# Eight special dk stores instead of five, with their rows dealt to chosen DMA engines

## The chip, the cores and the metric

The kernel runs on one core of one Trainium2 chip. The core has a matrix engine (PE, with weight loads shown apart as PEld), three engines for elementwise work (DVE, ACT, POOL), a synchronising engine (SP) and 16 DMA engines that move data between HBM and the on-chip memory. The metric is the time of one execution in microseconds (us); lower is better. Before the change it was 1268.67 us, the median of 3 runs from 1267.47 to 1269.34 us.

## The reference

The computation is the decode step of attention with its gradients, for 2 x 32 = 64 heads. A head has one query row of 128, and 8192 rows of keys and of values, all in bf16.

```python
scale = q.shape[-1] ** -0.5
scores = einsum("bhqd,bhkd->bhqk", q, k) * scale      # q (2,32,1,128), k and v (2,32,8192,128)
p = softmax(scores, axis=-1)
out = einsum("bhqk,bhkd->bhqd", p, v)
dq, dk, dv = vjp(out)(grad_out)
```

Written out for one head, with g the row of grad_out: dv is the outer product of p and g; dS = p * (V g - sum(p * V g)); dq is scale * dS K; dk is the outer product of dS and scale * q. So K and V (2 MB each for a head) are read once, and dK and dV (2 MB each) are written once: 256 transfers of 2 MB in all, nearly 537 MB.

## The kernel before

**Tiles.** A head's K, and its V, is one on-chip tile of 128 partitions with 64 rows of 128 numbers in each: 16,384 bytes a partition, contiguous in HBM. There are 12 such buffers, six heads deep. `load` (L106) brings a tile in on SP's DMA queue. The tile is read by PE and then overwritten in place by its own gradient: `outer` (L469) writes a quarter of it at a time with one DVE instruction (L475, a quarter is 16 of the 64 rows of each partition), and after the last quarter the tile is stored to dk or dv. The load for the head six places on, into the same buffer, waits for that store to land.

**Order of the work.** One loop (L506) makes eight steps a head, four quarters of K and then four of V, and interleaves up to four heads: transposes and scores of one head, softmax and sums of the one before, the outer products of the one before that. The order on every engine is pinned by hand. Within a head the dV quarters come first and the dK quarters right behind them.

**Queues.** Loads go out on SP's queue (q1 in the profile, hardware descriptors). Stores of whole tiles go out on POOL's queue (q0, software descriptors); only those of the last head go, a quarter at a time, on SP's. The final `out` and `dq` rows go on SP's (L585). In the trace the loads count their landings on eight semaphores in turn and POOL's DMAs on eight others, and a DMA whose semaphore is still owed a landing is not issued until that has come. A DMA posts sixteen landings, one an engine.

**Special stores.** Five of the 64 dk stores, those of heads 6, 17, 28, 39 and 50 (`SPREAD`, L23), are not sent as one DMA. `by_rows` (L96) sends partitions 8 to 127 first (120 rows of 16,384 bytes, with an upper bound on the length of the innermost piece, "cut") and then partitions 0 to 2, 3 to 5 and 6 to 7 (uncut). After the dv store of the next head, `turn` (L88) is called twice (`BACK`, L524): `turn(0)` resets a cursor of POOL's DMA queue, and `turn(5)` issues a tiny DMA of 5 rows of 16 bytes into a scrap tile (`parts_all`). The same is done once at the start (L128): a reset, and the first 5 query rows on POOL's queue. The cursor says on which DMA engine the next cut DMA of this queue begins.

**What the change touches** are the tables `SPREAD` and `BACK` at L23 to L26, the count of scrap tiles `NTURN` at L120 and the two calls of `turn` at L525 and L526.

Of the kernel before, what the change touches and what calls it, by code (L numbers as in the profile page):

```python
# [19 lines left out]
SW = 32  # L20
NTILE = 12
FIRST = 5
SPREAD = {  # L23
    i: ((8, 128, True), (0, 3, False), (3, 6, False), (6, 8, False)) for i in range(6, 56, 11)
}
BACK = {i + 1: FIRST for i in SPREAD}  # L26

@with_exitstack
def kernel(  # L30
# [57 lines left out]
    def turn(n):  # L88

        if n:  # L90
            parts = turns.pop()
            pin(store_eng.dma_start(out=parts[:n, :], in_=q_rows[:n, : 2 * QT], max_dma_last_dim=2 * QT))
        else:
            pin(store_eng.inc_swdge_sem([], [], mode="reset_dge_cursor"))

    def by_rows(dst, src, steps):  # L96

        for step in steps:
            if len(step) == 1:
                turn(*step)  # L100
                continue
            p0, p1, cut = step
            cap = {"max_dma_last_dim": NT * D} if cut else {}
            pin(store_eng.dma_start(out=dst[p0:p1], in_=src[p0:p1], **cap))

    def load(i, w, pieces=(NCH,)):  # L106
        h = heads[i]
        t = kvp.tile([P, NT, D], BF16, tag=f"kv{slot_of(i, w)}", name="kvt")
        h.tile[w] = t
        src = (v_v if w else k_v)[i]  # L110
        c = 0
        for m in pieces:
            n0, n1 = c * CH, (c + m) * CH
            pin(load_eng.dma_start(out=t[:, n0:n1, :], in_=src[:, n0:n1, :]))
            c += m
# [1 line left out]
    load(0, 0, (1, 1, 2))  # L117

    q_rows = q.rearrange("b h s d -> (b h s) d")
    NTURN = len(BACK) + sum(len(step) == 1 and step[0] > 0 for x in SPREAD.values() for step in x)  # L120
    parts_all = const.tile([CH, NTURN, 2 * QT], BF16, name="parts_all")
    turns = [parts_all[:, n, :] for n in range(NTURN)]

    qd_nat = evp.tile([P, CH, P], BF16, tag="ev", name="qd_nat")
    for w, a in enumerate((q, grad_out)):
        rows = a.rearrange("b h s d -> (b h s) d")
        r0 = FIRST if w == 0 else 0
        if r0:  # L128
# [73 lines left out]
    def begin(i):  # L202

        h = heads[i]
        sw = ps_sdp.tile([P, 2 * NT + 2 * P + 4], F32, tag="s", name="sw")
        h.score = (sw[:, 0:NT], sw[:, NT : 2 * NT])
        h.s, h.dp = h.score
        h.mT = sw[0:1, 2 * NT : 2 * NT + P]
        h.qbp = sw[:, 2 * NT + P : 2 * NT + 2 * P]
        h.lsum = sw[:, 2 * NT + 2 * P : 2 * NT + 2 * P + 2]  # L210
        h.mb = sw[:, 2 * NT + 2 * P + 2 : 2 * NT + 2 * P + 3]

    def window(i, w):

        pin(nc.scalar.copy(out=qwin[:, w, :, Q0 : Q0 + 2], in_=qpair[:, w, i]))

    def broadcast(i, w):

        h = heads[i]
        pin(  # L220
            nc.tensor.matmul(  # L221
                h.qbp,
                lhsT=qT[:, w, i : i + 1].to_broadcast([P, P]),
                rhs=ident_bf,
                start=True,
                stop=True,
            )
        )
        h.qb[w] = small.tile([P, D], BF16, tag=f"qb{w}", name="qb")
        pin(nc.vector.tensor_copy(out=h.qb[w][:], in_=h.qbp))  # L230

    def transpose_chunk(i, c):
        w, c = divmod(c, NCH)
        src = heads[i].tile[w]
        tp = ps_tp.tile([P, CH // 2, P], F32, tag="tp", name="tp")
        for m in range(CH // 2):
            n0 = c * CH + 2 * m
            two = src[:, n0 : n0 + 2, :].rearrange("p n d -> p (n d)").bitcast(F32)
            pin(nc.tensor.transpose(tp[:, m, :], two, ident_f[:]))  # L239
        ev = evp.tile([P, CH // 2, P], F32, tag="ev", name="ev")  # L240
        pin(nc.scalar.copy(out=ev[:], in_=tp[:]))  # L241
        return ev
# [26 lines left out]
    def keep_raw(i):  # L269

        h = heads[i]
        h.rows = work.tile([P, QT * P], F32, tag="rows", name="rows")
        pin(nc.vector.tensor_copy(out=h.rows[:], in_=h.raw[:]))  # L273
# [179 lines left out]
    def join(i, w):  # L453

        h = heads[i]
        pin(
            nc.tensor.matmul(h.acc[w][:, 0:1], lhsT=h.sel[:], rhs=ones[:], start=True, stop=True)  # L457
        )
        pin(
            nc.vector.tensor_scalar(  # L460
                out=(oT if w else dqT)[:, i : i + 1],
                in0=h.acc[w][:, 0:1],
                scalar1=h.rl if w else h.rls,
                scalar2=None,
                op0=ALU.mult,
            )
        )

    def outer(i, w, c, ends):  # L469

        h = heads[i]
        n0 = c * CH
        shape = [P, CH, D // 2, 2]
        pin(
            nc.vector.tensor_tensor(  # L475
                out=h.tile[w][:, n0 : n0 + CH, :].rearrange("p n (e t) -> p n e t", t=2),
                in0=h.qb[w][:]
                .rearrange("p (e t) -> p e t", t=2)
                .unsqueeze(1)
                .to_broadcast(shape),  # L480
                in1=h.pair[w][:, n0 : n0 + CH, :].unsqueeze(2).to_broadcast(shape),
                op=ALU.mult,
            )
        )
        if c + 1 in ends:
            at = ends.index(c + 1)
            b0, b1 = (ends[at - 1] if at else 0) * CH, (c + 1) * CH
            dst = (dv_v if w else dk_v)[i]
            if w == 0 and i in SPREAD:
                by_rows(dst, h.tile[w], SPREAD[i])  # L490
            else:
                eng = load_eng if len(ends) > 1 else store_eng
                pin(eng.dma_start(out=dst[:, b0:b1, :], in_=h.tile[w][:, b0:b1, :]))  # L493
# [12 lines left out]
    for g in range(SL * BH + O0 + NCH + 4 - SL):  # L506
        now = [(g // SL - b, g % SL + b * SL) for b in range(4)]
        now = [(i, r) for i, r in now if 0 <= i < BH]

        def at(r0):  # L510

            return next((i for i, r in now if r == r0), None)

        def within(r0):

            return next(((i, r - r0) for i, r in now if r0 <= r < r0 + NCH), None)

        if (i := at(O1 + NCH)) is not None and i + AHEAD < BH:
            load(i + AHEAD, 0)
        if (i := at(O0 + NCH)) is not None and i + AHEAD < BH:  # L520
            load(i + AHEAD, 1)
        if x := within(O1):
            outer(x[0], 1, x[1], last if x[0] == BH - 1 else whole)
        if (i := at(O1 + NCH)) in BACK:  # L524
            turn(0)  # L525
            turn(BACK[i])  # L526
        if x := within(O0):
            outer(x[0], 0, x[1], last if x[0] == BH - 1 else whole)
        ev = None
        if g < SL * BH:  # L530
            i, r = divmod(g, SL)
            if r == NCH:
                begin(i)
                broadcast(i, 1)
            if r == NCH + 2:
                broadcast(i, 0)
            ev = transpose_chunk(i, r)
        if (i := at(A1 + NCH + 2)) is not None:
            join(i, 1)
        if (i := at(A0 + NCH + 2)) is not None:  # L540
            join(i, 0)
        if x := within(A1):
            acc(x[0], 1, x[1])
        if x := within(A0):
            acc(x[0], 0, x[1])
        if (i := at(NCH + 1)) is not None:
            spread_rows(i, 0)
        if (i := at(SL + 1)) is not None:
            spread_rows(i, 1)
        if (i := at(NCH + 3)) is not None:  # L550
            max_spread(i)
            expo(i)
        if prev is not None:
            score_chunk(*prev)
        prev = (g // SL, g % SL, ev) if ev is not None else None
        if (i := at(NCH + 1)) is not None and i + 1 < BH:
            window(i + 1, 0)
        if (i := at(1)) is not None and i > 0:
            window(i, 1)

        if (i := at(NCH)) is not None:
            keep_raw(i)
        if (i := at(SL)) is not None:
            keep_raw(i)
        if (i := at(NCH + 1)) is not None:
            max_part(i)
        if (i := at(NCH + 2)) is not None:
            max_all(i)
        if (i := at(NCH + 4)) is not None:
            normalise_p(i)  # L570
        if (i := at(SL + 1)) is not None:
            weigh(i)
        if (i := at(SL + 2)) is not None:
            normalise_ds(i)
        if (i := at(A1 + NCH)) is not None:
            pick(i, 1)
        if (i := at(A0 + NCH)) is not None:
            pick(i, 0)
# [37 lines left out]
```

## Time and profile before

| | |
|---|---|
| runs | 1268.67 us (median of 3; 1267.47 to 1269.34) |
| profiled execution, its own time | 1267.85 us |
| its span, first to last instruction | 1266.1 us |
| busy: PE, DVE, ACT, POOL | 1187.7, 1031.3, 557.2, 80.6 us |
| bytes moved by DMA, mean rate | 538.53 MB, 425 GB/s |
| DMA packets on POOL's queue, on SP's queue | 19456, 20172 |
| mean granted clock of PE | 0.988 of full speed |

The page lists first how long every engine was busy. Then it cuts the span into 40 equal slices and shows for each the busy share in tenths, the granted PE clock, the mean busy share of the 16 DMA engines and what they moved in GB/s. Then come the DMA queues; the chain of work that ended last; the costliest groups of instructions, with the idle time before them and what ended it; and the DMA issues by line, with their size and the median time from issue to landing. Other views give the waits of each engine, the instructions of a stretch in order of time, and tables by stretch, in which the DMA share is a fraction of 1 (packets overlap by some nanoseconds, so that it can show 1.01). Behind the views stand the records of the trace: start, length, size and queue of every DMA packet, and the time of every landing. They don't name the engine, but an engine's packets follow one another without a break, so that each engine can be followed as a chain of packets.

### The profile page before, as it was taken

The page shows a single profiled execution, that of the slowest core. Times are in us where ns is not written, and L with a number is a line of the kernel's source. Part 1 is how long each engine was busy: PE and PEld are TensorE (multiplying, and loading weights), DVE is VectorE, ACT ScalarE, POOL GpSimd, SP SyncE. Part 2 cuts the span into 40 slices and gives each one's busy share as a digit, 9 for nine tenths or more (in the row PEclk, how much of TensorE's full clock was granted, in tenths as well). Part 3 has the DMA queues.
Part 4 walks back from the last instruction along what each step waited for, and adds up shares of the span by engine and source line. Part 5 has one row for each costly group of instructions (what it writes and reads, how often), then busy time and mean ns, then how long its engine had stood idle before and what let it go on. Part 6 is the DMA issues. An engine that isn't in the chain of part 4 may idle for free.

```text
span 1266.1 us, 24581 instructions
## 1 busy us (share of the span) xinstructions
PE 1187.7 (94%) x10056; PEld 783.1 (62%) x10056; DVE 1031.3 (81%) x2267; ACT 557.2 (44%) x769; POOL 80.6 (6%) x153
## 2 busy tenths in 40 slices
PE   6999999999999999999999999999999999999981
PEld 4666666666666666666666666666666666666650
DVE  3888888888888888888888888888888888887883
ACT  3444444444444444444444444444444444444430
POOL 0000010000010000001000001000000001000000
PEclk9999999999999999999999999999999999999995
DMA  9999999999999999999999999999999999999998
GB/s 393 422 429 429 429 428 429 429 429 429 430 429 428 429 429 429 429 429 429 423 428 430 430 429 428 428 427 430 429 430 428 429 429 427 429 429 429 429 430 336
DMA packets 39741, 538.53 MB, mean 425 GB/s; under 512 B 5236, under 2 KB 5236, under 8 KB 6516
## 3 DMA queue, kind: packets, MB, share of 16 engines
q1 hardware_dynamic: 20172, 272.70, 50.6%
q0 software_dynamic: 19456, 264.25, 49.1%
q8 instruction: 79, 1.29, 0.4%
q14 instruction: 34, 0.28, 0.1%
HBM read 268.47 MB, written 268.47 MB: 424 GB/s over the span
## 4 chain that ended last, share of the span: by engine, by line
PE 68%; DVE 16%; DMA 7%; another core or an unknown queue 4%; issue 2%; ACT 0%; SPq 0%; POOL 0%; ACTq 0%; DVEq 0%
PE tp L239 29%; PE acc L420 17%; PE raw L260 11%; DVE kvt L475 6%; PE sw L280 4%; DMA out_dram<-kvt 4%; DVE sel L443 4%; DVE rows L273 3%; DMA kvt<-in_v_dram 3%; PE sw L366 3%; PE sw L221 2%; PE sw L304 1%; DVE sel L437 1%; PE acc L457 1%
## 5 line engine op out<-in xcount | busy, mean ns | idle before, releaser
L241 ACT COPY ev<-tp 128x1024 f32<-128x1024 f32 x512 | 518.7, 1013 | 660.3 <-PE tp L239 654.8
L475 DVE TENSOR_TENSOR kvt<-qb,pair 128x2048 bf16<-128x2048 bf16 x512 | 617.2, 1216 | 0.2
L239 PE MATMUL tp<-ident_f,kvt 128*128 128x128 f32 x4096 | 547.6, 277 | 3.1 <-DMA kvt<-in_v_dram 2.6
L239 PEld LDWEIGHTS tp<-ident_f,kvt 128*128 128x128 f32 x4096 | 454.0, 144 | 84.2 <-issue 64.6
L260 PE MATMUL raw<-ev,qwin 128*32 128x512 bf16 x2048 | 209.5, 399 | 0.0
L420 PE MATMUL acc<-kvt,dS_pad 128*64 128x512 bf16 x1024 | 160.7, 395 | 0.8 <-DVE dS_pad L406 0.8
L420 PE MATMUL acc<-kvt,E_pad 128*64 128x512 bf16 x1024 | 159.5, 391 | 0.6 <-DVE E_pad L331 0.6
L280 PEld LDWEIGHTS sw<-sel,rows 128*128 128x128 f32 x1024 | 123.9, 191 | 52.4 <-DVE sel L443 25.9
L443 DVE SCALAR_TENSOR_TENSOR sel<-acc,diag,sel 128x128 f32<-128x128 f32 x384 | 134.7, 351 | 13.6
L260 PEld LDWEIGHTS <-qwin 128*32 128x32 bf16 x2048 | 52.7, 93 | 135.4 <-issue 131.0
L280 PE MATMUL sw<-sel,rows 128*128 128x16 f32 x1024 | 136.3, 265 | 0.0
L493 POOL DMA_DIRECT2D out_dram<-kvt x121 | 64.6, 533 | 1062.3 <-DVE kvt L475 484.4
L273 DVE COPY rows<-raw 128x512 f32<-128x512 f32 x128 | 88.6, 692 | 47.0 <-PE raw L260 47.0
L299 DVE TENSOR_REDUCE st<-sw 1x1 f32<-1x128 f32 x64 | 17.8, 278 | 55.9 <-PE sw L298 55.9
L221 PE MATMUL sw<-ident_f,qT 128*128 128x128 bf16 x128 | 28.9, 226 | 36.2 <-DVE st L294 36.2
L420 PEld LDWEIGHTS <-dS_pad 128*64 128x64 bf16 x1024 | 36.6, 108 | 34.9 <-issue 31.8
L366 PEld LDWEIGHTS sw<-st,ones 128*128 128x128 f32 x256 | 37.9, 186 | 31.0 <-issue 15.3
L420 PEld LDWEIGHTS <-E_pad 128*64 128x64 bf16 x1024 | 36.0, 108 | 33.6 <-issue 31.5
L366 PE MATMUL sw<-st,ones 128*128 128x1 f32 x256 | 48.8, 260 | 0.5 <-DVE st L337 0.5
L437 DVE TENSOR_SCALAR sel<-acc,diag 128x128 f32<-128x128 f32 x128 | 43.8, 342 | 0.0
L457 PEld LDWEIGHTS acc<-ones,sel 128*128 128x128 f32 x256 | 39.0, 193 | 7.2 <-DVE sel L443 7.2
L457 PE MATMUL acc<-ones,sel 128*128 128x1 f32 x256 | 36.7, 212 | 6.1 <-DVE sel L443 6.1
(54 smaller groups left out, 381.3 us busy)
## 6 DMA issues: line engine op xcount, KB each, us to landing
out_dram<-kvt POOLq DMA_DIRECT2D x121, 2048.0 KB, 44.9
kvt<-in_v_dram SPq DMA_DIRECT2D x64, 2048.0 KB, 20.1
kvt<-in_k_dram SPq DMA_DIRECT2D x63, 2048.0 KB, 20.2
out_dram<-kvt POOLq DMA_DIRECT2D x5, 1920.0 KB, 49.5
out_dram<-kvt SPq DMA_DIRECT2D x8, 512.0 KB, 20.1
kvt<-in_k_dram SPq DMA_DIRECT2D x2, 512.0 KB, 4.4
kvt<-in_k_dram SPq DMA_DIRECT2D x1, 1024.0 KB, 6.9
out_dram<-kvt POOLq DMA_DIRECT2D x10, 48.0 KB, 49.1
```

What stands on the lines that cost most here:

```text
L239: pin(nc.tensor.transpose(tp[:, m, :], two, ident_f[:]))
L241: pin(nc.scalar.copy(out=ev[:], in_=tp[:]))
L260: nc.tensor.matmul(h.raw[g * SW : (g + 1) * SW, :], lhsT=qwin[:, w, e, q0 : q0 + SW], rhs=cols[:, b, :, e], start=(c == 0), stop=(c == NCH ...
L273: pin(nc.vector.tensor_copy(out=h.rows[:], in_=h.raw[:]))
L280: nc.tensor.matmul(h.score[w].rearrange("p (n m t) -> p n m t", m=QT, t=2)[:, :, m, :], lhsT=h.rows[:, m * P : (m + 1) * P], rhs=sel4[:].r ...
L366: nc.tensor.matmul(out, lhsT=ones[:].to_broadcast([P, P]), rhs=col, start=True, stop=True)
L420: nc.tensor.matmul(h.acc[w][g : g + CW, :], lhsT=wts[:, n0 : n0 + CW], rhs=rows[:, n0 : n0 + QT, :].rearrange("p n d -> p (n d)"), start=( ...
L437: nc.vector.tensor_scalar(out=h.sel[:], in0=block, scalar1=diag[:, 0:1], scalar2=None, op0=ALU.mult)
L443: nc.vector.scalar_tensor_tensor(out=h.sel[:], in0=block, scalar=diag[:, b : b + 1], in1=h.sel[:], op0=ALU.mult, op1=ALU.add,)
L457: nc.tensor.matmul(h.acc[w][:, 0:1], lhsT=h.sel[:], rhs=ones[:], start=True, stop=True)
L475: nc.vector.tensor_tensor(out=h.tile[w][:, n0 : n0 + CH, :].rearrange("p n (e t) -> p n e t", t=2), in0=h.qb[w][:] .rearrange("p (e t) -> ...
L493: pin(eng.dma_start(out=dst[:, b0:b1, :], in_=h.tile[w][:, b0:b1, :]))
```

## The change

Eight dk stores are special, those of heads 6, 14, 22, 29, 35, 41, 47 and 53. They come in four forms. Heads 6 and 22 keep the old form. Heads 14 and 41 send 120 rows, a scrap DMA of 4 rows, and the other 8 rows as one cut DMA. Heads 29, 35 and 47 send 104 rows, a scrap DMA of 4, 15 or 11 rows, 17 rows as one cut DMA, and the last 7 rows as uncut pieces of 3, 3 and 1. Head 53 sends 104 rows and three uncut pieces of 8. After the following head's dv store there is a scrap DMA of a listed number of rows (none after head 53); the reset of the cursor is left in one place, behind head 6. The description of the change gives the aim: four stores as 120 rows without engine 4, four as 104 rows without three neighbouring engines, and the 17 rows on engine 7, 8 or 15.

```diff
+SMALL = ((0, 3, False), (3, 6, False), (6, 8, False))
+REST = ((17, 20, False), (20, 23, False), (23, 24, False))
 SPREAD = {
-    i: ((8, 128, True), (0, 3, False), (3, 6, False), (6, 8, False)) for i in range(6, 56, 11)
+    6: ((8, 128, True),) + SMALL,
+    14: ((8, 128, True), (4,), (0, 8, True)),
+    22: ((8, 128, True),) + SMALL,
+    29: ((24, 128, True), (4,), (0, 17, True)) + REST,
+    35: ((0, 104, True), (15,), (104, 121, True), (121, 124, False), (124, 127, False), (127, 128, False)),
+    41: ((8, 128, True), (4,), (0, 8, True)),
+    47: ((24, 128, True), (11,), (0, 17, True)) + REST,
+    53: ((0, 104, True), (104, 112, False), (112, 120, False), (120, 128, False)),
 }
-BACK = {i + 1: FIRST for i in SPREAD}
+BACK = {7: (0, 5), 15: (5,), 23: (2,), 30: (4,), 36: (12,), 42: (7,), 48: (15,)}
...
-    NTURN = len(BACK) + sum(len(step) == 1 and step[0] > 0 for x in SPREAD.values() for step in x)
+    NTURN = sum(n > 0 for x in BACK.values() for n in x) + sum(
+        len(step) == 1 and step[0] > 0 for x in SPREAD.values() for step in x
+    )
...
         if (i := at(O1 + NCH)) in BACK:
-            turn(0)
-            turn(BACK[i])
+            for n in BACK[i]:
+                turn(n)
```

## The prediction

> **What bounds the kernel now.** I read the busy slices and the DMA queues first.
>
> ```profile
> span 1266.1 us, 24581 instructions
> ...
> DMA  9999999999999999999999999999999999999998
> GB/s 393 422 429 429 429 428 429 429 429 429 430 429 428 429 429 429 429 429 429 423 428 430 430 429 428 428 427 430 429 430 428 429 429 427 429 429 429 429 430 336
> ...
> q1 hardware_dynamic: 20172, 272.70, 50.6%
> q0 software_dynamic: 19456, 264.25, 49.1%
> ```
>
> The DMA engines are busy in every slice and move 428 to 430 GB/s in nearly all; PE is the next fullest with 94%. Then the table by stretch, for the end:
>
> ```profile
> core 0: us, PE busy (x) PEld busy (x) DVE busy (x) ACT busy (x) POOL busy (x), PEclk, DMA share, GB/s
> 1000.00:1020.00 20.00, 19.43 (x168) 12.90 (x168) 17.02 (x37) 8.70 (x13) 1.06 (x2) 1.00 1.01 430
> 1020.00:1040.00 20.00, 19.43 (x168) 13.07 (x168) 17.02 (x39) 8.86 (x13) 0.64 (x1) 1.00 1.00 427
> 1040.00:1060.00 20.00, 19.43 (x168) 12.59 (x165) 16.77 (x37) 9.53 (x13) 1.09 (x2) 1.00 1.01 428
> 1060.00:1080.00 20.00, 19.43 (x168) 12.99 (x169) 16.85 (x40) 8.69 (x12) 2.65 (x5) 1.00 1.01 426
> ...
> 1220.00:1240.00 20.00, 14.81 (x112) 8.39 (x110) 17.38 (x39) 4.05 (x6) 0.54 (x2) 0.86 1.01 429
> 1240.00:1266.00 26.00, 3.36 (x14) 1.55 (x14) 6.25 (x12) 0.00 (x0) 0.00 (x0) 0.50 0.76 318
> ```
>
> All 16 engines work until 1240 us and only the last stretch has room (share 0.76), when PE and DVE have nothing left that matters. So the end is set by the DMA engine that finishes its own share last. How far apart do they finish? The landing records answer: a DMA posts one landing an engine, and those of the first `out_dram<-nat` transfer (16 KB behind everything else) came at 1251.0, 1251.6, 1251.8 | 1257.2 | 1259.8, 1259.8 | 1262.0, 1262.5, 1262.8, 1262.8, 1263.0, 1263.2, 1263.4, 1263.5, 1263.6, 1264.9 us. Their mean is 1260.2. The same bytes, dealt perfectly, would end 1264.9 - 1260.2 = 4.7 us earlier: that is all that dealing can win (0.37%).
>
> **Who is who.** An engine's packet of one row (16,384 bytes) is followed by the next 0.607 us after its start, in both queues; two half packets of a cut row take the same. So a row more or less is 0.607 us of an engine's end. At each old special store the packet records show fifteen engines with sixteen half rows, one with none, and three engines with one whole row from each uncut piece (two of them three rows in all, the third two), always among the five that also get a row of the 5-row scrap DMA. Row n of a scrap or uncut DMA therefore sits on engine n from its beginning, uncut ones begin at engine 0, and a cut DMA begins at the cursor and moves it on by the engines it used. Over the run the old tables moved 5 x 8 = 40 rows off engine 4 and put 15, 15 and 10 on engines 0, 1 and 2. That dates their ends: 15 x 0.607 = 9.1 and 10 x 0.607 = 6.1 us above the leading three at 1251.0 to 1251.8 gives 1260.1 to 1260.9 and 1257.1 to 1257.9, where the pair at 1259.8 and the single at 1257.2 are. So six engines have one natural speed: 0, 1, 2 and three that lead because they were given nothing. Ten are about 11 us slower over the run, engine 4 by some 24 us more, which its 40 rows repair. The records name a reason in part: the 79 instruction packets (q8, 1.29 MB) go round eight engines in turn, and in the stretches where I could follow them never to the three leaders. The names of these three are not in the trace: they are three of 5 to 15.
>
> **The change, part by part.** Following the cursor from 5: head 6 omits engine 4 as before; 14 omits 4 and puts one row each on 8 to 15; 22 omits 4; 29 omits 3, 4, 5 and puts 17 rows on 7; 35 omits 9, 10, 11 and puts 17 on 8; 41 is as 14; 47 omits 4, 5, 6 and puts 17 on 15; 53 omits 12, 13, 14 and puts three rows each on 0 to 7. These agree with the description of the change. Against the kernel before, in rows: engine 0 +3, 1 none, 2 +3, 3 -5, 4 -5, 5 -13, 6 -5, 7 +20, 8 +19, each of 9 to 14 -6, 15 +19; the sum is nought.
>
> Suppose 7, 8 and 15 are the three leaders. Then they end at 1251.0 to 1251.8 + 19 or 20 x 0.607 (11.5 or 12.1) = 1262.5 to 1263.9. The slow ten lose at least 5 rows, 3.0 us: at most 1261.9. Engines 0 and 1: at most 1259.8 + 1.8 = 1261.6. The leaders have become the last, about 4 us behind the mean of the ten, because 17 rows is more than the 13 or so that would level them.
>
> Empty shares: engines left out of a cut DMA still show a 4-byte packet for each piece they miss (the omitted engine of the old stores shows sixteen), 6 ns each. A 17-row DMA is 34 pieces, so 0.2 us for the others, three times; the leaders meet two of these, 0.4 us. The last end is then 1262.9 to 1264.3, say 1263.8 against 1264.9: 1.1 us less.
>
> POOL's issues: before, 20 special DMAs, 5 scrap DMAs and 5 resets; after, 36 within the special stores, 7 scrap DMAs behind them and 1 reset, while three whole stores more are replaced. That is 15 DMAs more at 0.51 to 0.64 us, under 10 us of POOL, which idles most of the span:
>
> ```profile
> POOL out_dram L493 <- DVE kvt L475: 484.4, 51, 13.4
> POOL out_dram L493 <- DVE qb L230: 475.5, 54, 34.3
> ...
> POOL out_dram L493 <- DMA out_dram<-kvt: 36.1, 4, 12.3
> POOL parts_all L92 <- DMA out_dram<-kvt: 25.8, 3, 8.9
> ...
> POOL out_dram L104 <- DMA out_dram<-kvt: 13.0, 3, 9.2
> ```
>
> The last three lines are what the issues do cost: a special store makes five DMAs of two, POOL's eight semaphores run out, and the stores behind wait for a landing (the queue's in order, so all of POOL's later stores, and through them SP's loads into those buffers, move back). At head 50 the following dk store went out at 1041.4 instead of about 1016.6 us. Yet the table above shows 426 to 430 GB/s there: each store takes 43.3 us (median) from issue to landing, so enough is queued. At heads 29, 35 and 47 the event has seven DMAs, two landings more, at 9.7 us each: about 25 + 19 = 44 us late, as long as the queue lasts. I take nothing for it; the ends are 0 (a store is still queued) and 2 us of idleness a time, 6 us in all. The fewer resets and 16-byte rows I take at nothing: a scrap DMA's packet is some 10 ns on an engine, times 12.
>
> Sum: -1.1 + 0, about 1267.85 - 1.1 = 1266.7 for a profiled execution; from the median of runs, 0.8 above it, 1267.6.
>
> **A rule against it.** The trace shows three engines of 5 to 15 ahead and doesn't name them. The Trainium skill, DMA: Bandwidth & Descriptors, section Latency and other measured facts, says that engines 7 and 15 are usually slower than 0-6 and 8-14; no row here shows that. By it, this change would load two of the slow ten, and the sum would be that of the first rival.
>
> **The rivals.** (1) *An engine fed 17 rows isn't a leader.* Then it ends at 1262.0 to 1264.9 + 11.5 or 12.1, that is 1273.5 to 1277.0, or 8.6 to 12.1 us later than now: 1277 to 1281, and any one of the three is enough. It decides as soon as one of them has now less than about 9 us of lead over the last (1264.9 + 2.5 - 11.6 = 1255.8). For it: nothing in the records names them. Against: engine 4 and engines 0 to 2 were treated by the old tables just as the ends call for, and ten engines are slow, exactly as many as the new table relieves (3 to 6, 9 to 14). (2) *POOL's semaphores starve the stores*, as priced: up to 6 us, 1267.6 to 1274, slower by over 0.2% from about 4 us on. Against it, the full rate around 1040 us. (3) *The 17 rows are not confined to one engine* but fall two by two on 0 to 8: engines 0 to 7 get six, engine 4 then -39 against -40, the last end moves by +0.6 us: about 1269.3. Against it, 120 and 5 rows went just where the cursor says. (4) *A better level*: if an ordinary run has the leaders further ahead than the profiled one, up to the 4.7 us: 1264 to 1266.
>
> **How the numbers follow.** 0.2% is 2.5 us, about what a measurement of this kernel can tell from no change. The forecast gets 0.57, rival 3 0.03 (both within 0.2%), rival 1 0.20, rival 2 0.07, rival 4 0.13. So faster 0.13, same 0.60, slower 0.27. The likeliest has 1266.0 to 1270.0 of its own; to leave out no more than 0.2 the range goes down to 1264.3 and up to 1278.0, into rival 1.
>
> **What would show it.** Right: three engines' landings of the last transfers move from 13 us ahead to the end of the field, the ten come 3 to 4 us earlier (engine 5 some 8), the spread shrinks from 13.9 to 5 to 9 us, and the share in the last stretch rises while the span shrinks by about 1 us. Wrong by rival 1: one to three landings stand some 10 us behind the rest. Wrong by rival 2: a slice between 640 and 1080 us falls under 420 GB/s, POOL waits over 20 us for a landing.

## The result and the profile after

The changed kernel takes 1282.02 us (median of 5 runs, 1281.36 to 1285.62) against 1267.47 us (5 runs, 1267.33 to 1269.34): a ratio of 1.0116, 95% interval 1.0100 to 1.0132. It is 14.5 us slower where 1.1 us less was forecast for the profiled execution and 1267.6 us for the median. The profiled execution has an own time of 1281.36 us and a span of 1279.6 us, 13.5 us more than before. The first lines to read are again the DMA slices and the queues:

```profile
span 1279.6 us, 24600 instructions
...
DMA  9999999999999999999999999999999899999997
GB/s 396 417 428 430 429 429 428 430 429 428 428 428 430 428 430 426 429 431 427 425 406 427 429 423 401 430 427 431 427 431 418 339 428 432 426 426 426 431 427 324
...
q1 hardware_dynamic: 20172, 272.70, 50.2%
q0 software_dynamic: 21936, 264.26, 48.9%
```

Each slice is 32.0 us. In the first twenty the rates are those of before; then there are four holes, 406, 401, 418 and 339 GB/s, in the slices that begin at 640, 768, 960 and 992 us. The bytes are the same, so the holes are lost time. The table by stretch (columns as before: busy time of each engine, granted clock, DMA share, GB/s) narrows them down:

```profile
640.00:660.00 20.00, 19.43 (x168) 12.87 (x166) 17.01 (x39) 9.07 (x13) 2.69 (x5) 1.00 0.95 389
...
760.00:780.00 20.00, 19.43 (x168) 12.75 (x166) 16.98 (x38) 8.90 (x13) 2.24 (x5) 1.00 0.98 404
780.00:800.00 20.00, 19.43 (x169) 13.00 (x165) 16.94 (x39) 9.55 (x14) 2.04 (x4) 1.00 0.99 399
...
1000.00:1020.00 20.00, 19.43 (x169) 12.56 (x167) 17.01 (x36) 9.20 (x13) 3.79 (x7) 1.00 0.78 303
1020.00:1040.00 20.00, 17.88 (x140) 11.61 (x136) 14.56 (x33) 7.25 (x10) 1.06 (x2) 0.91 1.00 423
...
1240.00:1279.60 39.60, 10.74 (x52) 5.15 (x48) 16.11 (x36) 0.00 (x0) 0.53 (x1) 0.52 0.82 343
```

PE is as busy as ever in the holes (19.43 of 20 us), so it isn't a late PE that starves the stores; the DMA engines have nothing to do for part of the time. (From 780 to 800 us, with a share of 0.99, they are at work nearly throughout, and some packets take longer.) The holes lie 40 to 80 us behind the stores of heads 29, 35 and 47 (those of 29 and 47 begin at 598 and 943 us), the three events with seven DMAs (an event is a special store with its scrap DMAs). POOL's waits for landings:

```profile
POOL out_dram L113 <- DMA out_dram<-kvt: 90.8, 12, 9.2
...
POOL parts_all L101 <- DMA out_dram<-kvt: 32.4, 4, 8.9
POOL out_dram L504 <- DMA out_dram<-kvt: 29.6, 6, 9.4
POOL out_dram L504 <- DMA parts_all<-in_q_dram: 18.8, 2, 12.5
```

They are 172 us in 24 waits against 75 us in 10 before. In order of time, POOL's instructions around head 47's event (start, busy time, line and operation, and in brackets the idle time before it and what ended it):

```profile
943.22 0.77 POOL L113 DMA_DIRECT2D out_dram<-kvt  x1 [9.87 <-DVE kvt L486]
943.98 0.58 POOL L101 DMA_DIRECT2D parts_all<-in_q_dram  x1
952.77 0.96 POOL L113 DMA_DIRECT2D out_dram<-kvt  x1 [8.22 <-DMA out_dram<-kvt]
962.54 0.56 POOL L113 DMA_DIRECT2D out_dram<-kvt  x1 [8.80 <-DMA out_dram<-kvt]
972.22 0.54 POOL L113 DMA_DIRECT2D out_dram<-kvt  x1 [9.12 <-DMA out_dram<-kvt]
981.97 0.51 POOL L113 DMA_DIRECT2D out_dram<-kvt  x1 [9.22 <-DMA out_dram<-kvt]
991.95 0.55 POOL L504 DMA_DIRECT2D out_dram<-kvt  x1 [9.46 <-DVE qb L241]
1001.43 0.60 POOL L101 DMA_DIRECT2D parts_all<-in_q_dram  x1 [8.94 <-DMA out_dram<-kvt]
1013.99 3.20 POOL L504 DMA_DIRECT2D out_dram<-kvt  x6 [11.95 <-DVE st L305]
```

From 943 to 1014 us POOL issues one large store, at 991.95, besides the event's own 104 rows; undisturbed it issues one every 9 to 10 us. At 1013.99 six come at once. The wait before them is put down to DVE, but DVE's work had gone on all along. The landing records show what it was: the six DMAs of the special store, issued from 943.2 to 982.0 us, are all complete only between 1013.4 and 1014.5 us. The first of them had landed on 15 engines by 1000.8 us; the sixteenth came at 1013.4.

Why they land together is in the same records. A semaphore is released when the last of the 16 engines has landed. Before, a store's last landing comes 1.5 to 5.2 us after the one ahead of it (medians of 60 us stretches from 640 us on). After, it comes 16.4 us later around 820 to 880 us and still 15.0 around 940 to 1000: one engine is far behind all others, and everything on POOL waits for it. From about 1008 to 1016 us the queues are all but dry (DMA share 0.44), and the 16 engines stand still for 5.4 us on average between 980 and 1040 us.

The whole loss, from the DMA packet records of the two profiled executions (us, mean of 16 engines):

| | before | after | difference |
|---|---|---|---|
| idle, from 20 us to 40 us before the end | 0.3 | 7.6 | +7.3 |
| packets longer than nominal (0.607 us for 16 KB, half for 8 KB) | 6.6 | 11.1 | +4.5 |
| 4-byte and other tiny packets, 6 ns each | 2.0 | 2.8 | +0.8 |
| idle in the last 40 us | 6.4 | 7.5 | +1.1 |
| sum | | | +13.7 |
| span | 1266.1 | 1279.6 | +13.5 |

### The profile page after: what moved, and what is told of

Read it like the earlier page. It is cut to its first block, busy times and chain, and to the rows that moved or that the text cites. A ratio compares the mean times of both kernels' runs of the same rounds, so it can differ in the third digit from the quotient of the medians.

```text
span 1279.6 us, 24600 instructions
## 1 busy us (share of the span) xinstructions
PE 1194.3 (93%) x10056; PEld 786.5 (61%) x10056; DVE 1031.5 (81%) x2267; ACT 556.9 (44%) x769; POOL 91.5 (7%) x168
## 4 chain that ended last, share of the span: by engine, by line
PE 66%; DMA 15%; DVE 15%; issue 2%; another core or an unknown queue 1%; ACT 0%; SPq 0%; POOL 0%; DVEq 0%; ACTq 0%
PE tp L250 28%; PE acc L431 16%; PE raw L271 10%; DMA kvt<-in_v_dram 9%; DVE kvt L486 6%; PE sw L291 4%; DMA parts_all<-in_q_dram 4%; DVE sel L454 3%; DVE rows L284 3%; PE sw L377 3%; DMA kvt<-in_k_dram 2%; PE sw L232 2%; PE sw L315 1%; DVE sel L448 1%
```

## Experiments

Two theories went in. **S**: POOL's eight semaphores run out behind an event of seven DMAs, the stores behind it come late and the DMA engines run dry. **L**: 17 rows put on one engine make it lag, and whatever waits for a full landing waits for it. Each kernel's ratio is against the kernel before on the same chip, with its 95% interval. "Long packets" below leaves out the first 100 us, which vary by up to 3 us between executions for no reason that the records show: before 5.0 us, after 9.1.

**The changed kernel again**, on another chip.

> The changed kernel itself on the chip of these runs, as their measure: 1280 to 1284 us by every theory.

Measured: 1284.81 us, 1.0116 (1.0092 to 1.0140); idle in mid-run 8.0 us. The loss is stable, and so is its place: there too one engine lands its stores 15 to 16 us after the next from about 820 to 1000 us.

**Five DMAs instead of seven, 17 rows kept.**

```diff
-REST = ((17, 20, False), (20, 23, False), (23, 24, False))
+REST = ((17, 24, False),)
...
-    35: ((0, 104, True), (15,), (104, 121, True), (121, 124, False), (124, 127, False), (127, 128, False)),
+    35: ((0, 104, True), (15,), (104, 121, True), (121, 128, False)),
```

> The changed kernel, but at heads 29, 35 and 47 the last seven rows go as one uncut DMA in place of three (3, 3 and 1): two DMAs fewer in each event, five in place of seven, and the 17 rows stay on engines 7, 8 and 15. Theory S (POOL's eight semaphores run out, stores are missing and the DMA engines idle): most of the 14 us goes, 1267 to 1272 us, and the mid-run idleness of the DMA engines (7.6 us an engine in the changed kernel, between 20 us and 40 us before the end) falls under 2 us. Theory L (17 rows on one engine put it some 20 us behind, and all landings wait for it): 1278 us or more, the stretch 1000 to 1020 us stays under 400 GB/s.

Measured: 1273.00 us, 1.0048 (1.0031 to 1.0065). Two DMAs fewer at three events win back some 9 of 14 us. Its profiled execution was the slowest of ten (1281.72 us), so its span is not compared; its idle time in mid-run is 1.4 us though one engine lags there by up to 17 us too. The edit also deals the seven rows to engines 0 to 6, three rows more for each of 3 to 6 over the run (1.8 us), which does not favour S. S holds for the larger part; lag without full semaphores leaves the engines busy.

**Seven DMAs, but 16 rows, one for each engine, instead of 17 on one.**

```diff
-REST = ((17, 20, False), (20, 23, False), (23, 24, False))
+REST = ((16, 19, False), (19, 22, False), (22, 24, False))
...
-    29: ((24, 128, True), (4,), (0, 17, True)) + REST,
+    29: ((24, 128, True), (4,), (0, 16, True)) + REST,
...
-BACK = {7: (0, 5), 15: (5,), 23: (2,), 30: (4,), 36: (12,), 42: (7,), 48: (15,)}
+BACK = {7: (0, 5), 15: (5,), 23: (2,), 30: (5,), 36: (13,), 42: (7,), 48: (16,)}
```

> The changed kernel, but the 17 rows of heads 29, 35 and 47 are 16 rows, one on each of the 16 engines, with uncut pieces of 3, 3 and 2 behind them; the scrap DMAs are altered so that later stores begin on the same engines. As many DMAs as in the changed kernel, no engine with 17 rows. Theory S: still slow, 1274 to 1282 us, with stretches under 410 GB/s behind these heads. Theory L: 1265 to 1270 us and no such stretch.

Measured: 1277.85 us, 1.0081 (1.0058 to 1.0104). The rates on its page, and two lines of its table by stretch:

```profile
GB/s 352 429 430 428 430 427 431 427 431 426 431 427 431 427 431 421 426 430 428 429 390 429 429 425 399 427 431 425 428 429 428 418 428 429 428 420 429 428 427 320
```

```profile
640.00:660.00 20.00, 19.43 (x168) 12.90 (x168) 17.01 (x36) 8.69 (x12) 2.68 (x5) 1.00 0.95 382
...
1000.00:1020.00 20.00, 19.43 (x170) 13.16 (x167) 16.92 (x38) 8.90 (x13) 3.77 (x7) 1.00 1.00 413
```

The holes behind heads 29 and 35 are there without any lagging engine, so S needs no help for them. The large hole behind head 47 (303 GB/s) has become 413, with the engines at work all through (share 1.00): that one was S and L together. Idle in mid-run is 3.2 us instead of 7.6.

**Five DMAs and 16 rows**, both edits at once.

```diff
-REST = ((17, 20, False), (20, 23, False), (23, 24, False))
+REST = ((16, 24, False),)
...
-    47: ((24, 128, True), (11,), (0, 17, True)) + REST,
+    47: ((24, 128, True), (11,), (0, 16, True)) + REST,
...
```

> The changed kernel with both edits: 16 rows, one on each engine, in place of 17 on one, and the last eight rows as one uncut DMA: five DMAs in an event, no engine with 17 rows. If the 5.3 us that were left with five DMAs and 17 rows (1273.0) come from the 17 rows lagging on one engine: 1267 to 1269 us. If they come from the number of events and the six heads between them (11 before): 1271 to 1274 us.

Measured: 1274.58 us, 1.0053 (1.0035 to 1.0070), idle in mid-run 0.5 us. The four make a square:

| ratio to before | seven DMAs | five DMAs |
|---|---|---|
| 17 rows on one engine | 1.0116 (twice) | 1.0048 |
| 16 rows, one each | 1.0081 | 1.0053 |

With five DMAs the lag costs nothing that shows; with seven it adds about 0.35% or 4 us (the intervals of 1.0116 and 1.0081 just overlap; the mid-run idleness, 7.6 against 3.2 us, says the same). With no lag and no idleness 0.5% still remain, some 6.6 us.

**The uncut pieces on SP's queue**, so that POOL has fewer DMAs to wait for.

```diff
-            pin(store_eng.dma_start(out=dst[p0:p1], in_=src[p0:p1], **cap))
+            eng = store_eng if cut else load_eng
+            pin(eng.dma_start(out=dst[p0:p1], in_=src[p0:p1], **cap))
```

> The changed kernel with its uncut pieces issued on SP's queue in place of POOL's; every row stays on the engine it had. POOL's queue has three DMAs fewer in each event of heads 29, 35 and 47 (four in place of seven, scrap DMAs included). Theory S (POOL's eight semaphores run out): 1266 to 1270 us, no stretch under 420 GB/s behind these heads, mid-run idleness of the DMA engines under 1 us an engine. A rival to it, theory R (the stores that pass over the ends of the engines, 104 and 17 rows, are themselves what breaks the stream, however many DMAs): 1272 us or more, as with five DMAs (1273.0).

Measured: 1275.41 us, 1.0051 (1.0037 to 1.0065). Idle in mid-run falls to 0.4 us and POOL's waits for landings to 77 us, as S wants; but the time is not the 1266 to 1270 us of S, it lies where theory R put it (R: the stores of 104 and 17 rows break the stream by themselves). What remains can't be read as the price of those stores, since the same move costs the kernel before 0.56% (two steps below), and the old deal at eight events, further down, has no such store and loses as much.

**The kernel before with two scrap DMAs more at three events** (seven DMAs, no row moved).

```diff
+SPREAD |= {
+    i: ((8, 128, True), (16,), (16,), (0, 3, False), (3, 6, False), (6, 8, False)) for i in (28, 39, 50)
+}
```

> The kernel before, with two more scrap DMAs (16 rows of 16 bytes, one on each engine) behind the first piece of the special stores of heads 28, 39 and 50; rows dealt as before. Theory S: the five DMAs of these events become seven, idleness of 2 to 9 us an engine in all, 1270 to 1278 us. Theory L: nothing changes, 1266.5 to 1269.5 us.

Measured: 1271.75 us, 1.0033 (1.0018 to 1.0049). Its rates:

```profile
GB/s 363 424 429 428 429 429 429 430 429 428 431 428 427 430 429 428 429 428 429 409 424 429 430 429 429 427 418 430 428 429 429 429 428 423 429 429 430 429 429 361
```

Two DMAs that carry 16 rows of some bytes open holes of 409 and 418 GB/s in a kernel that had none. That is S by itself, at a third of the price, with events eleven heads apart. The idleness is 1.4 us, under the 2 to 9 forecast; 1.3 us more are longer packets.

**The kernel before with 17 rows on engine 8 at one event**, five DMAs.

```diff
+SPREAD[39] = ((24, 128, True), (4,), (0, 17, True), (17, 24, False))
+BACK = {i + 1: FIRST for i in SPREAD} | {29: 7}
```

> The kernel before, with head 39's special store as 104 rows (omitting engines 4, 5, 6), a scrap DMA of 4 rows, 17 rows on engine 8 and seven uncut rows: four DMAs and one scrap DMA behind, as many as before. Theory S: within 1.5 us of the kernel before. Theory L: slower by 3 us or more, with one engine 6 to 20 us behind in the stores' landings after 840 us. If engine 8 is none of the three leaders, its last landing is some 10 us behind the others and the time 1274 to 1279 us.

Measured: 1268.81 us, 1.0005 (0.9995 to 1.0015). At this lag, 11 us behind the median, L alone costs nothing that shows. The run also names an engine. Around 800 us three engines land their stores well ahead of the median in this kernel (14.6, 13.0 and 11.4 us) as in the one before (14.6, 13.7, 13.3). From 880 to 920 us, behind head 39, the kernel before still has three (17.2, 16.3, 15.0) and its last engine 5.3 us behind; here two are 18.4 and 16.9 ahead, the next only 10.7, and the last is 11.3 behind. So engine 8 was one of the three leaders and has become the last, a shift of at least 22.7 us. That is over twice 17 x 0.607 = 10.3; my reading, which no run isolates, is that each store row on an engine also waits for a load row, so that a queue's landings shift by about twice the time of the rows.

**The kernel before with its uncut pieces on SP's queue** (the edit of two steps above).

> The kernel before with the uncut pieces of its five special stores on SP's queue: two DMAs of POOL's queue in an event in place of five. Theory S: POOL no longer waits for a landing; the time falls by 0 to 1 us, since the engines hardly idled (0.3 us each in mid-run), 1266.5 to 1268 us. Theory R: the same.

Measured: 1275.09 us, 1.0056 (1.0041 to 1.0071). Both theories had 1266.5 to 1268 us. POOL no longer waits for any landing, and yet the kernel is slower. SP's queue in order of time, around head 17's event:

```profile
384.94 0.33 SPq L115 DMA_DIRECT2D kvt<-in_k_dram  x1
385.37 0.94 SPq L105 DMA_DIRECT2D out_dram<-kvt  x3
429.18 0.37 SPq L115 DMA_DIRECT2D kvt<-in_v_dram  x1
429.65 1.01 SPq L115 DMA_DIRECT2D kvt<-in_k_dram  x1
430.82 1.33 SPq L115 DMA_DIRECT2D kvt<-in_v_dram  x1
```

After three pieces SP issues no load for 43 us, then five in 5 us. Idle in mid-run is 1.1 us and in the last 40 us 10.7 instead of 6.4. The waits changed queue, from the stores to the loads.

What are the 6 us that stay? The next kernels ask whether the new deal of rows costs them, or the number of events, their closeness, or their DMAs.

**The old deal of rows, but eight events of five DMAs at the new heads**; three of them move no row.

```diff
-    i: ((8, 128, True), (0, 3, False), (3, 6, False), (6, 8, False)) for i in range(6, 56, 11)
-}
+    i: ((8, 128, True), (0, 3, False), (3, 6, False), (6, 8, False)) for i in (6, 22, 35, 47, 53)
+} | {i: ((0, 80, False), (80, 96, False), (96, 112, False), (112, 128, False)) for i in (14, 29, 41)}
```

> Asks what costs the 5 to 7 us that remained with five DMAs an event. Old deal of rows, unchanged: the old form moves to heads 6, 22, 35, 47 and 53, and three events that move no row are added at heads 14, 29 and 41 (80 + 16 + 16 + 16 uncut rows, then reset and 5 scrap rows), so that there are eight events of five DMAs 6 to 8 heads apart. If the number or closeness of the events costs them (each event holds up POOL's stores and shortens the queue), 1272 to 1275. If the new deal of rows costs them, 1266.5 to 1269.5.

Measured: 1275.44 us, 1.0066 (1.0037 to 1.0095). Lines of its page, and POOL's waits for landings:

```profile
span 1271.2 us, 24602 instructions
...
GB/s 394 421 429 429 430 428 428 429 430 429 426 427 429 430 429 424 428 430 428 427 419 429 429 425 425 428 428 416 428 427 427 403 428 429 426 424 427 429 431 341
```

```profile
POOL parts_all L92 <- DMA out_dram<-kvt: 47.5, 6, 8.9
POOL out_dram L493 <- DMA out_dram<-kvt: 44.3, 4, 13.3
POOL out_dram L104 <- DMA out_dram<-kvt: 37.4, 6, 9.2
```

With the rows dealt as before, the 0.5 to 0.7% are there all the same: they come from the events, not from the deal. Of the 5.1 us in the span of the profiled execution, one of the faster ones (the runs go from 1271.35 to 1282.72 us), 5.1 are longer packets; idle time in mid-run is 0.5 us and in the last 40 us 6.0. The slice at 403 GB/s lies where the engines are all busy (share 1.01 and 1.00 from 980 to 1020 us) and each does less.

**Five events, close together.**

```diff
-    i: ((8, 128, True), (0, 3, False), (3, 6, False), (6, 8, False)) for i in range(6, 56, 11)
+    i: ((8, 128, True), (0, 3, False), (3, 6, False), (6, 8, False)) for i in (29, 35, 41, 47, 53)
```

> The kernel before with its five events, unchanged in form, at heads 29, 35, 41, 47 and 53 in place of 6, 17, 28, 39 and 50. If closeness costs (an event meets a queue that has not recovered from the one before), 1270 to 1273 and a slice under 425 GB/s in the second half. If it is only the number of events, or only the deal, 1266.5 to 1269.5.

Measured: 1269.48 us, 1.0026 (1.0005 to 1.0048). Closeness costs little in most runs: 1.7 us between the medians. But three of the 11 runs took 1277.5 to 1279.3 us, so that the means are 3.4 us apart, and the interval reaches nearly to nothing. More than half of the loss with eight events (8.0 us between the means) needs the larger number.

**Eight events, three of them with three DMAs** (against the old deal at eight events).

```diff
-} | {i: ((0, 80, False), (80, 96, False), (96, 112, False), (112, 128, False)) for i in (14, 29, 41)}
+} | {i: ((0, 120, False), (120, 128, False)) for i in (14, 29, 41)}
```

> As the kernel with eight events of five DMAs and the old deal (1275.44), but the three events that move no row have three DMAs: 120 + 8 uncut rows, then reset and 5 scrap rows. If it is the number of DMAs in an event that costs, 1267 to 1271; if every event costs, whatever its size, 1273 to 1277.

Measured: 1272.73 us, 1.0041 (1.0028 to 1.0053), between the two forecasts and not told from the five-DMA form by the intervals. Of 6.3 us in the span, 4.3 are longer packets, 0.8 mid-run idleness and 1.0 the tail (the last 40 us).

**A deal with few DMAs**: seven events, 68 rows put 17 each on engines 15, 0, 1 and 2, 34 rows put 17 each on 7 and 8.

```diff
+LOW = ((8, 128, True), (0, 8, False))
+HIGH = ((8, 128, True), (4,), (0, 8, True))
+SPREAD = {
+    6: LOW,
+    14: HIGH,
+    21: ((0, 68, True), (68, 128, True)),
+    28: LOW,
+    35: ((3, 37, True), (37, 128, True), (0, 3, False)),
+    42: HIGH,
+    50: LOW,
+}
+BACK = {7: (1,), 15: (15,), 22: (3,), 29: (3,), 36: (15,), 43: (5,), 51: (1,)}
```

> A deal that loads the same engines 7, 8 and 15 but with few DMAs: seven events of two or three store DMAs and one scrap DMA, no reset. 68 rows as one cut DMA put 17 rows on each of 15, 0, 1, 2 and the other 60 rows go four each to fifteen engines; 34 rows put 17 on 7 and 8. Against the kernel before, in rows: 0 and 1 +1, 2 +2, 3 to 5 -2, 6 -9, 7 +8, 8 +7, 9 to 14 -3, 15 +14. By the rows alone the last end comes 1.2 to 1.8 us earlier. If DMAs per event are what costs (theory S), 1265 to 1268. If rows that lag behind on a few engines, or the number of events, cost by themselves, 1270 to 1275.

Measured: 1289.48 us, 1.0170 (1.0148 to 1.0191). One engine ends some 19 us behind the median, so this tells nothing of DMAs per event: the deal was not the one meant. The next kernel shows why.

**The kernel before with three DMAs an event and a 1-row scrap DMA for the cursor.**

```diff
+SPREAD = {i: ((8, 128, True), (0, 8, False)) for i in range(6, 56, 11)}
+BACK = {i + 1: (1,) for i in SPREAD}
```

> The kernel before with its five events cut from five DMAs and a reset to three DMAs (120 rows, one uncut piece of 8, one scrap row and no reset). The deal becomes worse by rows: 0 and 1 -10, 2 -5, 3 to 7 +5, so the last end moves by up to +3.0 us: 1268 to 1271 if the five DMAs of the old events cost nothing. If they do cost (POOL's 75 us of waits for landings), what they cost comes off that: 1265 to 1268. POOL's waits for landings fall from about 75 to under 25 us in either case.

Measured: 1292.55 us, 1.0198 (1.0178 to 1.0218); one engine ends 17 to 20 us behind the median. I had taken a 1-row DMA to move the cursor by one. If it doesn't, the cursor stays at the engine left out, 4, and the next events leave out 3, 2, 1 and 0: engine 4 is spared 8 rows instead of 40, and 32 x 0.607 = 19.4 us is what it ends late. But the trace has another reading. It records each of these 1-row DMAs as eight packets of 2 bytes (the row's eight numbers), which start up to 48 us apart behind the last event, as packets on one engine's queue would not. If it used eight engines and moved the cursor by eight, the events leave out 4, 11, 2, 9 and 0: engine 4 is again spared 8 rows of 40, and the 19.4 us are the same.

**The same two with a reset and 5 scrap rows instead of the 1-row DMA.** First the deal by 68 and 34 rows:

```diff
-BACK = {7: (1,), 15: (15,), 22: (3,), 29: (3,), 36: (15,), 43: (5,), 51: (1,)}
+BACK = {7: (0, 5), 15: (15,), 22: (3,), 29: (3,), 36: (15,), 43: (5,)}
```

> The deal by 68 and 34 rows again, with a reset and a 5-row scrap DMA behind head 7 and nothing behind head 51 in place of the 1-row scrap DMAs. If a 1-row DMA does not move the cursor, that alone made 1289 of this kernel: no engine stands 20 us behind at the end any more. Seven events of two or three store DMAs: 1264 to 1268 if DMAs per event are what costs; 1270 to 1275 if the events, or rows that lag on a few engines, cost by themselves.

Measured: 1275.96 us, 1.0063 (1.0050 to 1.0076). The lone engine is gone, so the 1-row DMA was the fault. POOL hardly waits for landings now:

```profile
POOL parts_all L100 <- DMA out_dram<-kvt: 17.7, 2, 8.9
POOL out_dram L112 <- DMA out_dram<-kvt: 5.2, 1, 5.2
```

That is 23 us, less than a third of before, and 0.4 us of idleness in mid-run; yet it loses 8 us. S is therefore not the whole story: 4.5 us are longer packets and 3.8 us a worse tail (10.2 us idle in the last 40). The deal also shows who leads. In the store before the 68-row DMA seven engines are 4 to 8 us ahead; in the landings of that DMA itself four stand together 9.9 to 12.4 us behind, 2.5 us apart, two are 10.6 ahead and one 3.4, so that the four came from the seven (in the stores after it they are 4, 9, 13 and 17 us behind). A slow engine among 15, 0, 1 and 2 would have stood some 8 us behind the others, so 15 is a leader with 0, 1 and 2.

And the kernel before with three DMAs an event:

```diff
-BACK = {i + 1: (1,) for i in SPREAD}
+BACK = {i + 1: (0, 5) for i in SPREAD}
```

> The kernel before with 120 rows, one uncut piece of 8, a reset and 5 scrap rows at its five events (three DMAs instead of five). The deal is worse by rows: 0 and 1 -10, 2 -5, 3 to 7 +5, so that the last end moves by up to +3.0 us: 1268 to 1271 if the five DMAs of the old events cost nothing, 1265 to 1268 if they cost something. No engine 20 us behind at the end, and POOL's waits for landings under 40 us.

Measured: 1273.63 us, 1.0045 (1.0032 to 1.0059), outside both forecasts; POOL's waits for landings, 61 us, fell less than forecast. Its 5.8 us of span are 3.1 in the tail, which is the 3.0 that the worse deal should cost, and 2.6 of longer packets.

Side by side, for the kernels whose events differ in number (us, mean of 16 engines, from the profiled executions):

| kernel | events | long packets | idle in mid-run |
|---|---|---|---|
| before | 5 | 5.0 | 0.3 |
| 5 close together | 5 | 5.8 | 0.3 |
| 17 rows once | 5 | 6.0 | 0.5 |
| two scrap DMAs more | 5 | 6.3 | 1.4 |
| before, three DMAs | 5 | 7.5 | 0.3 |
| five DMAs, 16 rows | 8 | 8.8 | 0.5 |
| old deal, eight events | 8 | 10.1 | 0.5 |
| old deal, three of them smaller | 8 | 9.1 | 1.0 |
| deal by 68 and 34 rows | 7 | 9.4 | 0.4 |
| after | 8 | 9.1 | 7.6 |
| before, three DMAs, 1-row scrap | 5 | 11.7 | 3.0 |
| deal by 68 and 34 rows, 1-row scrap | 7 | 13.1 | 1.3 |

Without a lone slow engine, seven or eight events have 8.8 to 10.1 us of longer packets, five have 5.0 to 7.5. The last two rows, each with one engine some 19 us late, have more whatever their events: the number of events isn't the only thing that lengthens packets. The long ones stand in clusters, most of them 40 to 80 us behind an event, in both queues (a half to two thirds are stores), while all 16 engines are at work. Why a packet takes longer there (mostly 0.9 to 1.1 us, the longest 2.8, instead of 0.607) isn't settled: it is neither the cut (the three events added to the old deal cut nothing), nor POOL's waits (the deal by 68 and 34 rows has few), nor a free engine. No kernel tried here beats the one before.

## Why the prediction was wrong

**What bounds the kernel** was right: the DMA engines' work and their gaps sum to the loss, and PE's and DVE's waits never come into it.

**The step that failed** is the one on POOL's issues. It saw the two landings more and about 44 us of delay at heads 29, 35 and 47, set that against the queue's 43.3 us, and then put "I take nothing for it", with an end of "2 us of idleness a time, 6 us in all". Measured: 7.3 us more idleness, about half of the loss, of which 5.4 at head 47 alone. Two things were missing. A delay as long as the queue is no cover: the sum had no margin, and the square of experiments shows holes from it with no lag at all. And the 9.7 us a landing was the rate of engines that stand level. The event itself sets one engine back, a semaphore waits for the last of 16, and so the landing that POOL waits for at the next event is the laggard's.

**A term that was not in the sum**: three more events. They were entered as "15 DMAs more" and "under 10 us of POOL" (POOL's busy time did rise, by 10.9 us), at nothing for the DMA engines. The old deal at eight events measures 1.0066, 7.6 us between the medians; the 5.1 us of its profiled execution are all longer packets.

**The deal of rows** was priced at -1.1 us. Landings of the first `out_dram<-nat` transfer after: 1267.8 and 1267.9, 1269.1, then 1271.9 to 1275.4, and a last one at 1278.3, mean 1272.6. The spread shrank from 13.9 to 10.5 us, near the 5 to 9 that were to show it right, but the last stands 5.8 us behind the mean instead of 4.7: +1.1 instead of -1.1. The reason is in the middle of the run. The three leaders were 13.1, 11.2 and 10.0 us ahead around 600 to 640 us. Behind the hole of head 29 the first three are 4.2, 4.0 and 3.8 ahead. The kernel with 16 rows, one on each engine, shows that this is the hole and not the 17 rows: there the first three go from 13.7, 11.9 and 10.4 us ahead to 2.5, 2.3 and 2.2. When the queue runs dry, the engines start again nearly level. A fast engine's lead exists only while work is queued, and the 17 rows were dealt for leads that were gone. So head 35's 17 rows put one engine 18.9 us behind the median by 800 to 840 us, where in the one-event experiment engine 8 ended up 11.3 us behind.

**Rival 1** (17 rows on an engine that isn't a leader) has its number, 1277 to 1281, near the result, but not its mechanism: 8 leads by the one-event experiment, 15 by the 68-row event, and 7 is left for the third by elimination. The packets support it: at 649.1 us, when all engines but one had landed the 104 rows of head 29, at most 8 of the 34 half rows of the 17-row DMA had yet to begin. An engine of the middle, free for them from 644.3 us, could have begun 16 by then at 0.30 us each, so the engine that takes them was ahead (the profiled run with five DMAs, the slowest of its ten, does not show this: 32 were left). The last engine does not end 10 us behind the rest. The rule of the Trainium skill, DMA: Bandwidth & Descriptors, section Latency and other measured facts, that 7 and 15 are usually slower, is contradicted here for 15 (ahead before the 68-row DMA) and not supported for 7. **Rival 2** was the mechanism, with 0.07 and at most 6 us. Both its signs came: slices at 406, 401, 418 and 339 GB/s, and POOL waiting 44 us for landings from 943 to 1002 us, though no single wait was longer than 12.5 us. Its price was low because it stopped at the first round of waiting; with the lag, and with the events' own cost, it is 14.5 us. **Rival 3** falls: rows that were not confined to one engine could not leave one engine 15 us behind the next. **Rival 4** saw no level gained.

That all engines were full around 1040 us in the kernel before was read as evidence against rival 2. It only said that five DMAs were covered. It did not say by how much.

## What to carry to other kernels

Where few semaphores guard a queue, small DMAs behind large ones cost a large landing each, and a delay about as long as the queue must be priced as idleness, not as covered. Balancing transfers by hand has a price per intervention: count the interventions as well as the rows, and expect any stretch in which the queue runs dry to wipe out the leads on which the balance was worked out. Here a deliberate lag on one engine cost nothing that showed while semaphores were free, and about 4 us when they were not, because a transfer is complete only with its slowest engine.

## What the runs showed that was not expected

- The last of the sixteen engines landed a store 16.4 us after the one ahead of it (median around 820 to 880 us), and each semaphore is held for all of that.
- 17 rows, 10.3 us of an engine's time, shifted that engine's store landings by at least 22.7 us against the others.
- A 1-row scrap DMA is recorded as eight packets of 2 bytes and does not leave the cursor where one row on one engine would: the kernel with it ended 25 us late, the same with a reset and 5 rows 6.4 us late.
- Taking all of POOL's 75 us of waits for landings away by moving three small DMAs an event to SP's queue made the kernel before 0.56% slower, since SP issued no load for 43 us after them.
- Packets of 16 KB took 0.9 to 1.1 us and up to 2.8 instead of 0.607 behind some events, with all 16 engines at work. What makes them long is open.
